# The last pass of a gated product: its weights read once in fp32 and split on the chip

## The chip, the cores and the metric

The kernel runs on one core of a Trainium2 chip. The metric is the device time of one execution in microseconds. Engines: TensorE (PE in the profile; its weight loads are PEld), VectorE (DVE), ScalarE (ACT), GpSimd (POOL) and SyncE (SP), whose queue issues nearly all transfers.

## The reference

Attention over 4 batches of 12 heads, 448 tokens, with the heads mixed before and after the softmax, gives x of 1792 tokens by 768. Then come two layers, everything in fp32:

```python
h = x @ w_in            # w_in: 768 x 2048
g = h - np.tanh(h)
x = g @ w_out           # w_out: 2048 x 768
# second layer: a softmax over tokens and over 32 slots, 8 experts of 768 x 1024 x 768
logits = x @ phi
slot_input = softmax_over_tokens(logits).T @ x
slot_out[e] = np.maximum(slot_input[e] @ w1[e], 0.0) @ w2[e]
out = softmax_over_slots(logits) @ slot_out
```

Inputs arrive as 64-bit words for some weights; the kernel converts `w_in` and `w_out` to fp32 on the chip and keeps them in DRAM as `wi` and `wo`.

## The kernel before, in words

**Stages.** `talking_heads` computes the attention and, beside it, converts the weights. `moe_and_slots` follows. Its stage 1 computes h transposed, 128 columns of `w_in` at a time (16 of them, `NF`), for four passes over the tokens (`PASS`, 512, 512, 512 and 256 tokens). One pair of pass and column block is a *unit* t, 0 to 63; the last pass is units 48 (`LAST`) to 63. The tail after it sums up slots and runs the experts.

**A unit.** `product` (lines 712 to 727) makes hp, 128 by 256 in the last pass, of 6 chunks c of 3 matmuls each (L722). fp32 is split into a rounded part h and a rest l, both in fp32r, for w and for x, and the three matmuls are hw·hx, lw·hx and hw·lx. So a unit needs w as 128 x 2 halves m x 2 parts x 384. In the first pass `split_w` makes the parts of `wi` on the chip (L683 ScalarE, L684 GpSimd) and `save_w` writes both to DRAM as `wis`, 768 KB a unit. The other passes read `wis` back.

**The gate.** `gate_act` (ScalarE: Square L741 into a PSUM bank `sq`, Square L742 into `qd`, Tanh L745 into `g`, Relu L746 into `mk`), `gate_first` (VectorE: L751 and L752 on `qd`, L753 on `g`) and `gate_last` (VectorE: L758 reads `qd` and writes hp, L759 copies hp into `g` under the mask). There is one `qd` and one `mk`; of `g` there are five. VectorE's L751 starts after ScalarE's Relu, since both read the bank `sq`. `turn_g` transposes g on TensorE (L780), a ScalarE copy (L783) takes it out of PSUM.

**The order.** The schedule is written by hand: each engine runs in the order in which the program issues. `step(t)` issues, for t above 2: the load of a later unit; `gate_act(t-1)`, between whose L742 and L745 a function (`beside`) is called; then `product(t)`, with hooks ahead of chunks: chunk 1 `gate_first(t-1)`, chunk 2 `turn_g(t-2)`, chunk 3 and 4 the work on logits and slots of the pass before (steps 49 to 53), chunk 4 `gate_last(t-1)`. The transposes of unit t-2 therefore stand a third of the way into unit t.

**The ring.** `ring` has four slots of 6 KB a partition: two in `rg`, one each in two tiles of a pool that is closed within the last pass (step 54), to make room for three expert homes `z`. Up to unit 47 slot t % 4 is used; `load_w(t + 3)` loads whole units (L674). In the last pass only t % 2 is left, and `load_half(t + 2, m)` (L678) reloads a half of the slot just read, ahead of chunk 3 and behind chunk 5, as soon as TensorE is through with it. Expert tiles of 1.5 MB are loaded into homes that come free; in the last pass they go in pieces, one `load_piece` (L656) a step, behind the halves on SP's queue. The rest is issued behind the last unit, and then homes follow as `give` finds them (L652): the ring, `xc`, the gate's tiles, then each expert tile that is used up.

Of the kernel before, what the change touches and what calls it, by code (L numbers as in the profile page):

```python
# [9 lines left out]
FP32 = mybir.dt.float32  # L10
F32R = mybir.dt.float32r
ACTF = mybir.ActivationFunctionType
ALU = mybir.AluOpType
# [7 lines left out]
PASS = (512, 512, 512, 256)  # L21
# [525 lines left out]
def moe_and_slots(tc, ident, xd, wi, wo, wo4, wis, consts, w1, w2, out, box):  # L547
    nc = tc.nc
    NT, DM = out.shape
    KD = DM // 128  # L550
    NF = len(wi)
# [6 lines left out]
    HALF = DM // 2  # L558
    FH = F1 // 2
    NPASS = len(PASS)  # L560
    NST = NPASS * NF
    TM = max(PASS)
# [9 lines left out]
    RU = 2 * DM  # L572
    GR = 5
    NX = 7
    LAST = NST - NF

    whole = ExitStack()
    firsts = ExitStack()
# [8 lines left out]
    def bank(tag, shape, name):  # L587
        return bank_pool[tag].tile(shape, FP32, tag=tag, name=name)

    def r32(ap):  # L590
        return ap.bitcast(F32R)
# [6 lines left out]
    rg = rgp.tile([128, 2 * RU], FP32, tag="rg", name="rg")  # L598
# [3 lines left out]
    ring = [w.rearrange("p (m h i) -> p m h i", m=2, h=2) for w in (rg[:, :RU], rg[:, RU:], *rgs)]  # L602

    def unit(t):
        return ring[t % 4 if t < LAST else t % 2]


    mem = {}
# [8 lines left out]
    def give(x, last=False):  # L617
        free.append((x, last))
        load_expert()
# [34 lines left out]
    def load_piece(n=1):  # L654
        for dst, src in pending[:n]:
            nc.sync.dma_start(out=dst, in_=src)  # L656
        del pending[:n]
# [10 lines left out]
        return take(("e", t), n)  # L668

    def load_w(t):  # L670
        if t < NF:
            nc.sync.dma_start(out=unit(t)[:, :, 1], in_=wi[t].rearrange("p (m i) -> p m i", m=2))
        elif t < NST:
            nc.sync.dma_start(out=unit(t), in_=wis[t % NF])  # L674

    def load_half(t, m):
        if t < NST:
            nc.sync.dma_start(out=unit(t)[:, m], in_=wis[t % NF][:, m])  # L678

    def split_w(t, eng):  # L680
        if t < NF:
            w = unit(t)
            nc.scalar.activation(out=r32(w[:, :, 0]), in_=w[:, :, 1], func=ACTF.Copy)  # L683
            eng.tensor_tensor(out=r32(w[:, :, 1]), in0=w[:, :, 1], in1=w[:, :, 0], op=ALU.subtract)  # L684

    def save_w(t):
        if t < NF:
            nc.scalar.dma_start(out=wis[t], in_=unit(t))
# [7 lines left out]
    def load_x(p):  # L696
        n = PASS[p]
        if p == NPASS - 1:
            xbuf[p] = mem["thp"].tile([128, XW], FP32, tag="x0", name="xc")
            dst = xbuf[p][:, KD * n:2 * KD * n]  # L700
        else:
            dst = xbuf[p % 2][1][:, :KD * n]
        nc.sync.dma_start(out=dst.rearrange("p (a s) -> p a s", a=KD), in_=xd[p])
# [25 lines left out]
    def temps_of(t):  # L729
        n = PASS[t // NF]  # L730
        if t < 2:
            part = [quad[:, i * n:(i + 1) * n] for i in range(4)]
            return part[0], part[1], part[2], part[3] if t else mem["g0"]
        return mem["sq"][t], mem["qd"][:, :n], mem["mk"][:, :n], mem["g"][t % GR][:, :n]

    def gate_act(t, beside=None):
        hp = hps[t]
        if t > 1:
            mem["sq"] = {t: bank(f"q{t % 2}", [128, PASS[t // NF]], "sq")}
        sq, qd, mk, g = temps_of(t)  # L740
        nc.scalar.activation(out=sq, in_=hp, func=ACTF.Square)  # L741
        nc.scalar.activation(out=qd, in_=sq, func=ACTF.Square, bias=tshift)  # L742
        if beside:
            beside()
        nc.scalar.activation(out=g, in_=hp, func=ACTF.Tanh)  # L745
        nc.scalar.activation(out=mk, in_=sq, func=ACTF.Relu, bias=tlimit, scale=-1.0)  # L746
# [12 lines left out]
        nc.vector.copy_predicated(out=g, mask=mk.bitcast(I32), data=hp)  # L759

    def g_of(t):
        return temps_of(t)[3] if t < 2 else mem["g"][t % GR][:, :PASS[t // NF]]

    turns = [0]

# [25 lines left out]
    def load_o(f):  # L791
        if f < NF:
            nc.sync.dma_start(out=mem["wo"][f % NG], in_=wo[f])
# [45 lines left out]
    def mix_t(b):  # L839
        xt = bank("lg", [128, PASS[b]], "lT")  # L840
        nc.tensor.matmul(xt, lhsT=sel.rearrange("p g s -> p (g s)"), rhs=lp[b], start=True, stop=True)
        lg[b] = xt
# [7 lines left out]
    def slot_exp(b):  # L850
        xt = lg.pop(b)
        nm = keep.tile([128, 1], FP32, tag="nm", name="nm")
        ng = keep.tile([128, 1], FP32, tag="ng", name="ng")
        et = keep.tile([128, TM], FP32, tag="et", name="et")[:, :PASS[b]]
        sb = keep.tile([128, 1], FP32, tag="sb", name="sb")
        a = None
        nc.vector.tensor_reduce(out=nm, in_=xt, op=ALU.max, axis=AX.X)
        if b:
            nc.vector.tensor_tensor(out=nm, in0=nm, in1=run_m, op=ALU.max)
        nc.vector.tensor_scalar(out=ng, in0=nm, scalar1=-1.0, scalar2=None, op0=ALU.mult)  # L860
        nc.scalar.activation(out=et, in_=xt, func=ACTF.Exp, bias=ng, accum_out=sb)
        if b:
            a = keep.tile([128, 1], FP32, tag="al", name="al")
            nc.scalar.activation(out=a, in_=run_m, func=ACTF.Exp, bias=ng)
        es_in[b] = (a, et)
        runs[b] = (nm, sb)
# [59 lines left out]
    for n in range(3, NF + 1):  # L926
        m = 3 if n in (3, 4, 14, 15) else 2
        pieces[n], todo = todo[:m], todo[m:]

    def step(t):  # L930
        b, f = divmod(t, NF)
        hooks = {}

        def on(c, fn, *a):
            hooks.setdefault(c, []).append(lambda: fn(*a))

        if t < LAST:
            if 2 < t < LAST - 1:
                load_w(t + 3)
        else:  # L940
            on(KD // 2, load_half, t + 2, 0)
            on(KD, load_half, t + 2, 1)
        for n, hf in pieces.get(t - 1, []):
            if hf:
                load_o(n + NG)
        if t > 2:
            gate_act(t - 1, lambda: split_w(t + 1, nc.gpsimd))
        else:
            split_w(t + 1, nc.gpsimd)
        u = t - 2  # L950
        ws = pieces.get(t, [])
        if ws:
            on(1, turn_w, *ws[0])
        if t > 2:
            on(1, gate_first, t - 1)
        on(2, turn_g, u)
        if ws:
            on(3, turn_w, *ws[1])
        if b == 0:
            on(1, save_w, t)  # L960
        if b and f == 1:
            on(3, logits, b - 1, NQ - 1)
            on(4, logits_out, b - 1)
        if b and f == 2:
            hooks[1] = [lambda: mix_t(b - 1), lambda: slot_exp(b - 1)] + hooks[1]
            on(3, mix_n, b - 1)
            on(KD, slot_run, b - 1)
            on(KD, gates_first, b - 1)
        if b and f == 3:
            on(4, slot_turn, b - 1)  # L970
            on(KD, gates_last, b - 1)
        if b and f in (4, 5):
            on(3, slot_sum, b - 1, 2 * f - 8, 2 * f - 6)
        if t > 2:
            on(4, gate_last, t - 1)
        if b + 1 < NPASS:
            if f == 6:
                load_x(b + 1)
            if 8 <= f < 8 + KD:
                on(4, split_x, b + 1, f - 8)  # L980
        if len(ws) > 2:
            on(KD - 1, turn_w, *ws[2])
        if t in folds:
            on(KD - 1, fold_first)
            on(KD, fold_last, folds[t])
        if u % NG == NG - 1 and u % NF < NF - 1:
            on(KD, logits, u // NF, u % NF // NG)
        product(t, hooks)
        if b == 1 and f % 2 == 1 and f // 2 < NX:
            give(mem["ex"][f // 2], f // 2 == NX - 1)  # L990
        if b == 1 and f == NF - 1:
            give(mem["thp"].tile([128, EXB], FP32, tag="x1", name="ex"))
        if b == NPASS - 2 and f == NF - 1:
            mem["slow"] = True
            for l in range(2):
                give(xap.tile([128, EXB], FP32, tag=f"x{l}", name="ex"))
        if b == NPASS - 1:
            if f == 6:
                firsts.close()
                zp = whole.enter_context(tc.tile_pool(name="m_z", bufs=1, reuse_waits="tile"))  # L1000
                for i in range(3):
                    give(zp.tile([128, EXB], FP32, tag=f"z{i}", name="ex"))
            load_piece()
# [40 lines left out]
    tmp = temps.enter_context(tc.tile_pool(name="m_tmp", bufs=1, side="right", reuse_waits="tile"))  # L1044
# [2 lines left out]
    xbuf[1] = [thp.tile([128, XW], FP32, tag=f"x{l}", name="xb") for l in range(2)]  # L1047
    mem["SA"] = mids.tile([128, FB], FP32, tag="SA", name="SA")
    mem["ex"] = [mids.tile([128, EXB], FP32, tag=f"ex{i}", name="ex") for i in range(NX)]
    mem["g"] = [tmp.tile([128, TM], FP32, tag=f"g{i}", name="g") for i in range(GR)]  # L1050
    mem["qd"] = tmp.tile([128, TM], FP32, tag="qd", name="qd")
    mem["mk"] = tmp.tile([128, TM], FP32, tag="mk", name="mk")
    mem["wo"] = [mem["ex"][0][:, i * DM:(i + 1) * DM] for i in range(NG)]
# [9 lines left out]
    t = NST  # L1063
# [22 lines left out]
    tmp = whole.enter_context(tc.tile_pool(name="m_tz", bufs=1, side="right", reuse_waits="tile"))  # L1086
# [271 lines left out]
```

## Time and profile before

| | us |
|---|---|
| median of 3 runs | 939.89 |
| lowest, highest | 939.65, 943.64 |
| the profiled execution | 942.47 |
| its span, first to last instruction | 940.7 |

The profile shows one execution. Its rows name a line, an engine, an operation and the program's tiles; times are microseconds from the start of the span unless they are said to be ns. An idle time of an engine carries the event that ended it.

### The profile page before, as it was taken

How to read it: one execution, taken by the hardware profiler on the slowest of the kernel's cores; microseconds unless marked ns; L12 is line 12 of the kernel's file. 1: busy time of each engine (PE TensorE's matmuls, PEld its weight loads, DVE VectorE, ACT ScalarE, POOL GpSimd, SP SyncE). 2: the span in 40 equal slices, each digit the busy share in tenths (PEclk: the TensorE clock that was granted, in tenths of full speed). 3: DMA queues.
4: the chain of work that ended last, by engine and by line, in shares of the span. 5: the costliest groups of instructions: out<-in, count | busy, mean ns of one | idle time of the engine just before them, and what ended most of it. 6: DMA issues, size and time to landing. Idle time of an engine off the chain costs nothing.

```text
span 940.7 us, 19311 instructions
## 1 busy us (share of the span) xinstructions
PE 899.0 (96%) x6926; PEld 659.9 (70%) x6926; DVE 560.4 (60%) x1251; ACT 567.7 (60%) x1283; POOL 265.2 (28%) x467
## 2 busy tenths in 40 slices
PE   8799999999999999999999999999999989799985
PEld 6567777777777777777778777767776767665532
DVE  4376767767677666686555667557766775530103
ACT  4687767767777777777566576545664665521013
POOL 1364445544446444565432222000000000000000
PEclk9999999999999999999999999999999999999987
DMA  6986678976789766795368878669754438999997
GB/s 140 231 224 196 206 212 227 242 217 187 208 229 243 235 183 196 207 249 179 134 222 255 316 239 280 239 252 352 302 201 168 168 123 267 366 394 421 425 388 266
DMA packets 143858, 230.22 MB, mean 245 GB/s; under 512 B 60884, under 2 KB 121364, under 8 KB 139924
## 3 DMA queue, kind: packets, MB, share of 16 engines
q1 hardware_dynamic: 140416, 216.13, 71.4%
q10 hardware_dynamic: 3348, 12.87, 3.5%
q8 instruction: 56, 0.92, 0.4%
q14 instruction: 38, 0.31, 0.1%
HBM read 154.25 MB, written 36.18 MB: 202 GB/s over the span
## 4 chain that ended last, share of the span: by engine, by line
PE 83%; DMA 10%; ACT 2%; DVE 2%; issue 1%; SPq 1%; POOL 0%; ACTq 0%; POOLq 0%; DVEq 0%
PE hp L722 23%; PE pm L297 15%; PE tm L333 14%; PE vx L351 8%; PE sc L266 7%; DMA D<-S 4%; DMA ex<-in_moe_w_dram 3%; PE gt L780 2%; DMA rg<-wis 2%; PE so L1185 2%; PE h L1146 1%; PE lgp L830 1%; PE sp L912 1%; PE wt L799 1%; PE tz L1164 1%
## 5 line engine op out<-in xcount | busy, mean ns | idle before, releaser
L333 PEld LDWEIGHTS tm<-wk,e 120*112 120x112 f32 (+1 forms) x1440 | 174.8, 178 | 71.1 <-issue 59.8
L299 DVE TENSOR_REDUCE mx<-pm 120x1 f32<-120x448 f32 x180 | 112.1, 623 | 133.7 <-PE pm L297 133.2
L297 PE MATMUL pm<-D,wpre 120*120 120x448 f32 x360 | 174.9, 568 | 10.2 <-DMA D<-S 9.7
L336 ACT ACTIVATE aT<-tm 112x480 f32<-112x480 f32 x180 | 105.4, 585 | 123.4 <-PE tm L333 123.4
L333 PE MATMUL tm<-wk,e 120*112 120x120 f32 (+1 forms) x1440 | 177.5, 267 | 1.0 <-POOL wk L323 1.0
L323 POOL TENSOR_SCALAR wk<-wpost,rv 120x120 f32<-120x120 f32 x180 | 125.6, 698 | 142.5 <-PE tm L333 116.9
L722 PE MATMUL hp<-xa,rg 128*128 128x512 f32 x576 | 152.5, 405 | 0.0
L722 PEld LDWEIGHTS hp<-xa,rg 128*128 128x128 f32 x576 | 102.4, 188 | 28.5 <-issue 10.7
L306 ACT ACTIVATE e<-pm,mx 120x448 f32<-120x448 f32 x180 | 113.5, 630 | 6.2 <-DVE rv L318 3.3
L274 ACT ACTIVATE S<-sc 120x448 f32<-120x448 f32 (+1 forms) x186 | 90.8, 544 | 8.3 <-DMA D<-S 3.7
L1157 POOL MEMSET tq<- 128x256 f32 x8 | 2.4, 312 | 315.8 <-PE sip L1125 267.8
L751 DVE SCALAR_TENSOR_TENSOR qd<-qd,sq 128x512 f32<-128x512 f32 (+1 forms) x62 | 38.3, 618 | 83.1 <-ACT mk L746 83.1
L741 ACT ACTIVATE sq<-hp 128x512 f32<-128x512 f32 (+1 forms) x62 | 32.7, 527 | 88.1 <-PE hp L722 88.1
L351 PE MATMUL vx<-aT,vn 112*64 112x120 f32 (+1 forms) x1536 | 84.0, 262 | 0.0
L351 PEld LDWEIGHTS vx<-aT,vn 112*64 112x64 f32 x1536 | 73.9, 137 | 6.2 <-issue 0.9
L297 PEld LDWEIGHTS pm<-D,wpre 120*120 120x120 f32 x360 | 51.4, 182 | 33.3 <-issue 14.3
L722 PE MATMUL hp<-xb,rg 128*128 128x512 f32 x288 | 74.7, 404 | 0.0
L312 POOL TENSOR_SCALAR rv<-ss 120x1 f32<-120x1 f32 x180 | 43.0, 239 | 97.5 <-ACT e L306 87.9
L266 PE MATMUL sc<-khi,qT 64*120 64x448 f32 (+1 forms) x384 | 69.0, 388 | 0.8 <-DVE qT L249 0.8
L68 POOL TENSOR_TENSOR fa<-fa,f 128x384 f32<-128x384 f32 x64 | 65.5, 1024 | 5.3 <-issue 0.2
L722 PEld LDWEIGHTS hp<-xb,rg 128*128 128x128 f32 x288 | 52.0, 188 | 16.6 <-issue 6.3
L722 PE MATMUL hp<-xc,rg 128*128 128x256 f32 x288 | 42.5, 293 | 6.0 <-DMA rg<-wis 6.0
(163 smaller groups left out, 1317.2 us busy)
## 6 DMA issues: line engine op xcount, KB each, us to landing
ex<-in_moe_w_dram SPq DMA_DIRECT2D x25, 1536.0 KB
D<-S SPq DMA_DIRECT2D x172, 210.0 KB
rg<-wis SPq DMA_DIRECT2D x34, 768.0 KB
f<-in_moe_w_in_dram SPq DMA_DIRECT2D x32, 384.0 KB
f<-in_moe_w_out_dram SPq DMA_DIRECT2D x32, 384.0 KB
wis<-rg ACTq DMA_DIRECT2D x16, 768.0 KB
rg<-wis SPq DMA_DIRECT2D x28, 384.0 KB
wi<-fa SPq DMA_DIRECT2D x32, 192.0 KB
```

What stands on the lines that cost most here:

```text
L68: eng.tensor_tensor(out=out, in0=bits(a), in1=bits(p), op=ALU.add)
L266: nc.tensor.matmul(xs[e][0][:ni], lhsT=qT[n][s, l, p, :ni], rhs=kt[s], start=(i == 0), stop=(i == 2))
L274: nc.scalar.activation(out=dst, in_=xs[e][0][:ni], func=ACTF.Copy)
L297: nc.tensor.matmul(x[:r], lhsT=wpre[:r, :m, :], rhs=D_t.pop(s)[:r], start=True, stop=True)
L299: nc.vector.tensor_reduce(out=mx[:r], in_=x[:r], op=ALU.max, axis=AX.X, negate=True)
L306: nc.scalar.activation(out=e[:r], in_=pp_t.pop(s)[:r], func=ACTF.Exp, bias=mx_t.pop(s)[:r], accum_out=ss[:r])
L312: nc.gpsimd.tensor_scalar(out=rv[:r], in0=ss_t.pop(s)[:r], scalar1=EPS, scalar2=None, op0=ALU.add)
L323: nc.gpsimd.tensor_scalar(out=wk[:r], in0=wpost[:r], scalar1=ss_t.pop(s)[:r], scalar2=None, op0=ALU.mult)
L333: nc.tensor.matmul(x[:, c, :, :m], lhsT=e[:r, c * JP:(c + 1) * JP], rhs=wk[:r, :, :m], start=True, stop=True)
L336: nc.scalar.activation(out=attn_t[n][:, :, :, c0:c0 + m], in_=x[:, :, :, :m], func=ACTF.Copy)
L351: nc.tensor.matmul(x[64 * e:64 * e + 64, i, :ni], lhsT=nat_v[b, h // NP][:, h % NP, c, :], rhs=a[:, c, h, :ni], start=(c == 0), stop=(c == ...
L722: nc.tensor.matmul(hp, lhsT=r32(w[:, m, hl, cs]), rhs=r32(x_of(b, c, l)), start=(c == 0 and i == 0), stop=(c == KD - 1 and i == 2))
```

## The change

In the last pass w is loaded as fp32 from `wi`, into the place of the l part, and split per half: half 0 by ScalarE (a Copy to fp32r) between L742 and Tanh of the step before the product, half 1 by VectorE (a copy to fp32r) ahead of chunk 3 of that step; for both halves GpSimd then subtracts in place. Up to unit 54 (below `THREE` = 55) the four slots stay in use and whole units are loaded three steps ahead; from unit 55 there are three slots: the two of `rg` and one in the place of three `g` tiles, and halves are loaded three units ahead. The `g` tiles of the last pass lie in the other two `g` tiles and in the free half of `qd`.

```diff
+    THREE = LAST + 7
     def unit(t):
-        return ring[t % 4 if t < LAST else t % 2]
+        return ring[t % 4] if t < THREE else ring[(4, 0, 1)[(t - THREE) % 3]]
     def load_w(t):
-        if t < NF:
-            nc.sync.dma_start(out=unit(t)[:, :, 1], in_=wi[t].rearrange("p (m i) -> p m i", m=2))
-        elif t < NST:
+        if t == THREE:
+            ring.append(mem["tmp"].tile([128, RU], FP32, tag="gl", name="rg").rearrange(
+                "p (m h i) -> p m h i", m=2, h=2))
+        if t < NF or t >= LAST:
+            nc.sync.dma_start(out=unit(t)[:, :, 1], in_=wi[t % NF].rearrange("p (m i) -> p m i", m=2))
+        else:
             nc.sync.dma_start(out=unit(t), in_=wis[t % NF])
     def load_half(t, m):
         if t < NST:
-            nc.sync.dma_start(out=unit(t)[:, m], in_=wis[t % NF][:, m])
+            nc.sync.dma_start(out=unit(t)[:, m, 1], in_=wi[t % NF][:, m * HALF:(m + 1) * HALF])
+    def split_half(t, m):
+        if LAST <= t < NST:
+            h, l = unit(t)[:, m, 0], unit(t)[:, m, 1]
+            if m:
+                nc.vector.tensor_copy(out=r32(h), in_=l)
+            else:
+                nc.scalar.activation(out=r32(h), in_=l, func=ACTF.Copy)
+            nc.gpsimd.tensor_tensor(out=r32(l), in0=l, in1=h, op=ALU.subtract)
     def g_of(t):
-        return temps_of(t)[3] if t < 2 else mem["g"][t % GR][:, :PASS[t // NF]]
+        if t < 2:
+            return temps_of(t)[3]
+        if t < LAST:
+            return mem["g"][t % GR][:, :PASS[t // NF]]
+        i, n = (t - LAST) % GR, PASS[-1]
+        return mem["qd"][:, n:2 * n] if i == GR - 1 else mem["g"][3 + i // 2][:, i % 2 * n:(i % 2 + 1) * n]
     # in step(t)
-        if t < LAST:
-            if 2 < t < LAST - 1:
-                load_w(t + 3)
-        else:
-            on(KD // 2, load_half, t + 2, 0)
-            on(KD, load_half, t + 2, 1)
+        if 2 < t < THREE:
+            load_w(t + 3)
+        elif t >= THREE:
+            on(KD // 2, load_half, t + 3, 0)
+            on(KD, load_half, t + 3, 1)
-            gate_act(t - 1, lambda: split_w(t + 1, nc.gpsimd))
+            gate_act(t - 1, lambda: split_half(t + 1, 0) if t >= NF else split_w(t + 1, nc.gpsimd))
         on(2, turn_g, u)
+        on(3, split_half, t + 1, 1)
```

The five `g` tiles become slices of two tiles, `gl` (three) and `gh` (two), of the same size in all.

## Rows read from the trace of the kernel before

**Rows 1.** Busy time by stretches: us, PE, PEld, DVE, ACT, POOL, PEclk, DMA share, GB/s
```profile
770.00:828.00 58.00, 48.86 (x389) 40.32 (x388) 34.89 (x90) 30.06 (x83) 0.00 (x0) 1.00 0.89 308
798.00:828.00 30.00, 24.04 (x191) 21.26 (x190) 16.73 (x43) 16.14 (x44) 0.00 (x0) 1.00 0.99 360
840.00:900.00 60.00, 58.92 (x654) 32.73 (x658) 5.37 (x18) 7.61 (x15) 2.12 (x7) 1.00 1.01 423
...
910.00:915.00 5.00, 2.99 (x24) 0.68 (x16) 0.00 (x0) 0.00 (x0) 0.00 (x0) 0.52 1.07 374
```

**Rows 2.** Waits of PE and of ACT, 767 to 829 us: total, times, longest
```profile
PE hp L722 <- DMA rg<-wis: 6.0, 8, 1.5
...
ACT qd L742 <- DVE hp L758: 2.6, 3, 1.3
```

**Rows 3.** Timeline of ACT: start, us, what, idle before and what ended it
```profile
768.34 0.69 ACT L742 ACTIVATE qd<-sq,tshift 128x512 f32<-128x512 f32 x1
...
772.83 0.47 ACT L742 ACTIVATE qd<-sq,tshift 128x256 f32<-128x256 f32 x1 [1.29 <-DVE hp L758]
...
785.33 0.47 ACT L742 ACTIVATE qd<-sq,tshift 128x256 f32<-128x256 f32 x1 [0.96 <-DVE hp L758]
...
794.80 0.48 ACT L742 ACTIVATE qd<-sq,tshift 128x256 f32<-128x256 f32 x1
...
797.92 0.47 ACT L742 ACTIVATE qd<-sq,tshift 128x256 f32<-128x256 f32 x1
798.29 0.38 ACT L745 ACTIVATE g<-hp 128x256 f32<-128x256 f32 x1
...
800.71 0.48 ACT L742 ACTIVATE qd<-sq,tshift 128x256 f32<-128x256 f32 x1 [0.34 <-DVE hp L758]
...
828.81 0.47 ACT L742 ACTIVATE qd<-sq,tshift 128x256 f32<-128x256 f32 x1
```

**Rows 4.** Timeline of PE, one unit that waits for nothing
```profile
795.81 2.38 PE L722 MATMUL hp<-xc,rg 128*128 128x256 f32 x18
```

**Rows 5.** Transfers by form: queue, count, KB each
```profile
rg<-wis SPq DMA_DIRECT2D x28, 384.0 KB
...
ex<-in_moe_w_dram SPq DMA_DIRECT2D x12, 384.0 KB
...
ex<-in_moe_w_dram SPq DMA_DIRECT2D x6, 512.0 KB
```

**Rows 6.** Single lines, duration in ns: least/median/most, or busy us and mean
```profile
L707 ACT ACTIVATE xa<-xa x12: 622/630/653, 483.3 to 670.2; 128x512 fp32r<-128x512 f32 x12
...
L707 ACT ACTIVATE xc<-xc x6: 409/434/435, 731.1 to 755.6; 128x256 fp32r<-128x256 f32 x6
...
L1201 DVE CAST ex<-ceK x1: 391/391/391, 886.3 to 886.3; 128x448 fp32r<-128x448 f32 x1
...
L805 DVE COPY ex<-wt x16: 539/558/565, 509.6 to 594.0; 128x384 f32<-128x384 f32 x16
...
L68 POOL TENSOR_TENSOR fa<-fa,f x64: 1007/1018/1152, 51.4 to 459.0; 128x384 f32<-128x384 f32 x64
...
L51 DVE TENSOR_SCALAR fa<-fa x64: 341/353/1215, 39.9 to 451.7; 128x384 f32<-128x384 f32 x64
```

**Rows 7.** Timeline of DVE
```profile
767.50 0.69 DVE L758 SCALAR_TENSOR_TENSOR hp<-qd,hp 128x512 f32<-128x512 f32 x1
...
799.86 0.41 DVE L753 TENSOR_TENSOR g<-hp,g 128x256 f32<-128x256 f32 x1
800.19 0.42 DVE L758 SCALAR_TENSOR_TENSOR hp<-qd,hp 128x256 f32<-128x256 f32 x1
```

**Rows 8.** The chain that ended last: start, us, what
```profile
882.27 30.49 DMA ex<-in_moe_w_dram
```

**Rows 9.** Timeline of PE in the tail
```profile
912.89 2.79 PE L1185 MATMUL so<-ex,tq 128*32 128x384 f32 x16 [2.01 <-DMA ex<-in_moe_w_dram]
...
924.42 1.50 PE L1185 MATMUL so<-ex,tq 128*32 128x384 f32 x16
```

More of the change, by code (lines that the diff above doesn't have):

```diff
@@ L733, in temps_of @@
             return part[0], part[1], part[2], part[3] if t else mem["g0"]
-        return mem["sq"][t], mem["qd"][:, :n], mem["mk"][:, :n], mem["g"][t % GR][:, :n]
+        return mem["sq"][t], mem["qd"][:, :n], mem["mk"][:, :n], g_of(t)
     def gate_act(t, beside=None):
@@ L1049, in moe_and_slots @@
     mem["ex"] = [mids.tile([128, EXB], FP32, tag=f"ex{i}", name="ex") for i in range(NX)]
-    mem["g"] = [tmp.tile([128, TM], FP32, tag=f"g{i}", name="g") for i in range(GR)]
+    mem["tmp"] = tmp
+    gl = tmp.tile([128, 3 * TM], FP32, tag="gl", name="g")
+    gh = tmp.tile([128, 2 * TM], FP32, tag="gh", name="g")
+    mem["g"] = [gl[:, i * TM:(i + 1) * TM] for i in range(3)] + [gh[:, i * TM:(i + 1) * TM] for i in range(2)]
     mem["qd"] = tmp.tile([128, TM], FP32, tag="qd", name="qd")
```

## The prediction, made before the changed kernel was run

> **What bounds the kernel now.** I read the busy time by stretches first, then who waits for whom in the last pass of stage 1 (767 to 829 us), then the timelines of ScalarE, VectorE and TensorE there, then the end of the chain of waits.
>
> The stretches show a light and a heavy half of the last pass. From 798 to 828 us the DMA engines are busy 99% of the time at 360 GB/s, TensorE only 24.04 of 30 us; afterwards, from 840 to 900 us, DMA stays full at 423 GB/s [rows 1]. The waits name what the product lacks: TensorE stood 6.0 us, in 8 pieces, for ring loads from `wis` [rows 2]. That is what the change can remove from the pass directly.
>
> What is late next is in the same answer. ScalarE's second Square (L742, `qd`) waited three times for VectorE's L758, which reads `qd` last [rows 2]. There is one `qd`, so the gate is a loop: L742, Tanh, Relu on ScalarE, then L751, L752, L753, L758 on VectorE, then L742 of the next unit. The reader is to see the loop alone in ScalarE's timeline: L742 starts at 797.92 and, freed by L758, again at 800.71; so the bare loop takes **2.79 us** [rows 3]. The product itself takes 2.38 us for its 18 matmuls [rows 4]. Before, from the unit at 800.71 to the last at 828.81 (eight units), one unit took 28.10 / 8 = 3.51 us [rows 3]: the loop had 0.72 us to spare, because loads were slower still.
>
> **The change part by part.**
>
> *Loads.* 16 units of 768 KB become 384 KB: 6.3 MB less. Of ring halves and expert pieces, 28 x 384 KB, 12 x 384 KB and 6 x 512 KB are issued from 770 us on [rows 5], 18.87 MB; with the ring halves at 192 KB a unit brings 384 KB and about one piece of 384 to 512 KB, at most 0.92 MB, which 360 GB/s moves in 2.6 us. That is below both the old and the new time of a unit, and the third ring slot gives another unit of lead, so I take TensorE's 6.0 us for loads as gone. If that cover were gone, part of the 6.0 us would return.
>
> *First-half split.* ScalarE's Copy of 128x384 goes between L742 and Tanh, inside the loop. Copies from SBUF to fp32r take 630 ns for 512 columns and 434 for 256 [rows 6], so about 532 for 384. Consecutive operations overlap: L742 lasts 0.47 us, yet Tanh starts 0.37 after it [rows 3]. That takes off 0.10 to 0.11: **0.42 us** (bounds 0.37, the spacing of 256 columns, and 0.53).
>
> *Second-half split.* VectorE's copy stands between L753 and L758, in the loop too. The one cast to fp32r from SBUF takes 391 ns for 448 columns; a copy of 128x384 out of PSUM takes 558 [rows 6]. It is nearest the cast: about 0.36 for 384 columns. L753 lasts 0.41 and L758 starts 0.33 later [rows 7], so 0.08 comes off: **0.28 us** (bounds 0.26 and 0.48).
>
> *Subtractions.* GpSimd has two a unit of 128x384, 1.02 us each [rows 6], 2.04 in all, and nothing else. The first ends some 2.0 us after L742 starts, before the product wants that half; the second starts after VectorE's copy, about 3.1, and ends about 4.2, while TensorE, which waits for the gate (3.9) before its transposes, reaches that half's remainder near 4.7. I cost both at nothing; the cover is 0.5 us for the second. If it went, each microsecond beyond would be TensorE's.
>
> *Queues.* SP's loads per unit stay two or become one; they are behind the same TensorE events and carry the same expert pieces behind them. ScalarE's Tanh and Relu, and so all of VectorE's gate, are queued behind the Copy: that is the 0.42. L758 and the masked copy behind VectorE's copy: the 0.28. The extra ring slot is the old `g0` to `g2`, whose last readers run at step 49, while the load into it is issued at step 52: nothing. The first `z` home waits for unit 54, its piece is due at step 56: nothing.
>
> *The sum for the pass.* The loop becomes 2.79 + 0.42 + 0.28 = **3.49 us**, against 3.51 as loads paced it: the gain is spent. It also binds where the old pass was not short of data. L742 at 768.34 had 0.1 us to spare (L758 of the unit before ended at 767.50 + 0.69 = 768.19 [rows 7]), so 0.6 of 0.70 shows; at 772.83 it already waited for L758 (0.70 more) [rows 3]; after the logits ScalarE has to wait, before the next unit's gate, for VectorE's part of `gates_first`, which is queued behind one more copy, 0.28; and at 785.33 again a wait for L758 brings 0.70 [rows 3]. Sum 2.3 us. So L742 of unit 53, before at 794.80, comes at 797.1; nine spacings of 3.49 give 828.5 and the last gate, with no split behind it, 2.79 more: 831.3, against 828.81 before [rows 3]. **The pass ends 2.5 us later.** With 0.37 and 0.26 it is 1.9, with 0.53 and 0.48 it is 6.6.
>
> *The tail.* It is a stream of expert tiles. The chain ends through a tile issued at 882.27 that lands 30.49 us later [rows 8]; TensorE waits 2.01 us for it at 912.89, and the granted clock in 910 to 915 is 0.52, that is 1.2 GHz, after that idle time [rows 1, 9]. Homes for this stream open where the pass ends (the ring, `xc`, the gate's tiles are given out behind the last unit), so its start moves with the pass. What the lighter loads give is the backlog: 18.87 MB issued less 58 us x 308 GB/s = 17.86 moved by 828 [rows 1, 5] leaves 1.0 MB, 2.5 us at 400 GB/s. Bounds 0 and 2.5; I take 1.0, since a first transfer issued at the end of the pass doesn't flow at once, while a backlog covers that time.
>
> *Total:* 2.5 - 1.0 = **+1.5 us**. The profiled execution took 942.47 us (span 940.7, 1.8 around it), 2.6 above the median 939.89; it would become 944.0, the median **941.4**.
>
> **The rivals.**
>
> *A, slower: the copies cost their upper bounds.* Price: 6.6 - 1.0 = 5.6, 945.5 us. For it: the PSUM copy's 558 ns. Against: the cast's 391 [rows 6]. It decides from a VectorE copy of about 0.55 us on.
>
> *A', slower: VectorE's copy meets GpSimd's subtraction.* A one-input VectorE operation of 128x384 between SBUF operands, L51, has median 353 ns and once took 1215 [rows 6], in the stage where GpSimd works beside it. If each copy lost those 0.86 us, twelve loop-bound units would lose 10.3 more, 951.7 us. It decides if the first subtraction still runs when the copy's turn comes, 2.7 us after L742 starts; with 1.02 us it ends at 2.0, so I give this little. The Trainium skill, SBUF — State Buffer, section "SBUF: two separate sides", says that VectorE in a two-port mode and GpSimd take a port pair exclusively, for a whole instruction. By that rule, the long L51 is explained and the margin of 0.7 us is what protects this change; no row before shows a cast beside a subtraction.
>
> *B, a little faster: the tail's stall goes.* If the stream gains the 2 us that the tile at 912.89 is late, TensorE keeps 2.4 GHz: 2.0 us, and two groups of 16 matmuls take 1.50 instead of 2.79 us each [rows 9]: 4.6 less, 2.5 - 4.6 = -2.1, 937.8 us. Against it: 1.0 MB of backlog is barely enough.
>
> *C, clearly faster: the splits don't lengthen the loop.* Then loads and loop give 2.79 us a unit: ten from 794.80 end at 822.7 instead of 828.81, -6.1, with the backlog -7.1, 932.8 us. For it: ScalarE and VectorE each idle half of the pass. Against: idle time inside a loop is no room, and the order places both copies in it.
>
> *D: the change does not do what it says.* Loads stay late (latency, not bytes, set them). Then the old waits add to the loop only in part; it would end like A.
>
> **How the numbers follow.** Forecast 0.58, A and D 0.15, A' 0.04, B 0.14, C 0.09. A measurement here can tell about 0.5%, 4.7 us: 935.2 to 944.6. Faster by more: C and a third of B, 0.14. Slower: A, A', D and a small part of the forecast's upper end, 0.21. Same: 0.65. The range takes in B's 937.8 and A's 945.5 with a microsecond for each: 936.5 to 946.5; it leaves out C, A' and little else. The forecast's own range is 939 to 945.
>
> **What the profile after would show.** Right: no TensorE wait for ring loads after 798 us; DMA clearly below full there; L742 waiting for L758 in nearly every unit and spaced 3.4 to 3.6 us; TensorE standing for the gate (L759) before its transposes; the pass ending 2 to 3 us later; a wait for an expert tile near the end still there. Wrong: L742 spaced under 3.2 us or without that wait (C), VectorE's copies over 0.5 us (A) or some over 1 us (A'), or the granted clock staying at 2.4 GHz through the last `so` matmuls (B).

## The result and the profile after

| | before | after |
|---|---|---|
| median of 10 runs, us | 940.55 | 945.87 |
| lowest, highest | 936.45, 944.95 | 942.14, 949.67 |
| the profiled execution | 942.47 | 946.25 |
| its span | 940.7 | 944.4 |
| first to last product matmul of the last pass | 767.5 to 828.1: 60.6 | 770.1 to 835.5: 65.4 |
| behind it, to the end of the span | 112.6 | 108.9 |

The ratio of the times is **1.0054**, interval 1.0033 to 1.0076: 5.1 us slower, between 3.1 and 7.1 (the medians themselves lie 5.3 apart). The range 936.5 to 946.5 holds the 945.87; the forecast of 941.4 was 4.5 too low. It had added 1.5 us to a median of 939.89 of three runs, so as a forecast of the change alone it was 3.8 too low.

The two profiled executions differ ahead of the change too: the first product matmul of stage 1 starts at 490.3 us in one and at 492.8 in the other, and over all profiles of this study that start lies between 486.7 and 498.3, though no kernel differs there. So I compare the *pass*, the time from the first start of a product matmul on `xc` to the last, and not the spans. The pass took 4.8 us longer, about the whole loss.

The diff moves lines: L722 is now L735, L742 is L755, L745 L758, L758 L771, L759 L772, L780 L798, L783 L801, L830 L848, L859 L877, L893 L911, L912 L930, and L1185 L1206. The split's lines are L694 (VectorE), L696 (ScalarE) and L697 (GpSimd).

TensorE's product of the pass, by tile (count: least, median and most ns, first and last start):

```profile
L735 PE MATMUL hp<-xc,rg x288: 274/282/685, 770.1 to 835.5; 128*128 128x256 f32 x144
```

**Waits of TensorE after**, 760 to 840 us (total, times, longest):

```profile
PE gt L798 <- DVE g L772: 9.8, 12, 2.4
...
PE gt L798 <- ACT qd L755: 1.1, 1, 1.1
PE gt L798 <- DVE qd L772: 1.1, 1, 1.1
...
PE hp L735 <- POOL rg L697: 0.7, 1, 0.7
```

The 6.0 us for ring loads [rows 2] are gone from this list. In their place TensorE stands before the transposes for the gate. The same answer for the kernel before has, besides the loads:

```profile
PE gt L780 <- DVE g L759: 2.6, 3, 1.2
...
PE gt L780 <- ACT g L745: 1.8, 1, 1.8
```

The wait was not removed, it was exchanged: 6.0 for loads against 7.6 more for the gate (9.8, 1.1 and 1.1 against 2.6 and 1.8; `qd L772` is the gate of a unit whose g lies in the free half of `qd`) and 0.7 for a subtraction. What made the gate late stands in ScalarE's waits of the same stretch: `qd` waited 3 times and 2.6 us for VectorE [rows 2], now 12 times and 10.2.

```profile
ACT qd L755 <- DVE hp L771: 10.2, 12, 1.9
```

**ScalarE's timeline after** (start, us, what, the idle time before it and what ended it) shows the loop at its new length:

```profile
771.51 0.69 ACT L755 ACTIVATE qd<-sq,tshift 128x512 f32<-128x512 f32 x1 [0.66 <-DVE hp L771]
...
801.85 0.47 ACT L755 ACTIVATE qd<-sq,tshift 128x256 f32<-128x256 f32 x1
...
805.31 0.47 ACT L755 ACTIVATE qd<-sq,tshift 128x256 f32<-128x256 f32 x1 [0.37 <-DVE hp L771]
...
808.78 0.48 ACT L755 ACTIVATE qd<-sq,tshift 128x256 f32<-128x256 f32 x1 [0.69 <-DVE hp L771]
...
812.26 0.47 ACT L755 ACTIVATE qd<-sq,tshift 128x256 f32<-128x256 f32 x1 [0.68 <-DVE hp L771]
...
836.17 0.47 ACT L755 ACTIVATE qd<-sq,tshift 128x256 f32<-128x256 f32 x1
```

From unit 53 to unit 62 they come every 3.46 to 3.48 us (one of 3.75 apart), each freed by L771; the last, behind which no split stands, comes after 2.81. Against the pass's own start, `qd` of unit 53 stands at 31.8 us here (801.85 - 770.1), 27.3 before (794.80 - 767.5, [rows 3]): **of the 4.8 us, 4.5 are there by unit 53**, and from there on the two kernels run nearly level, one paced by the loop, the other by its loads.

**Busy time by stretches after** (us, PE, PEld, DVE, ACT, POOL, PEclk, DMA share, GB/s) locates the loss. DMA in the second half is at 0.76, where it was at 0.99 [rows 1]; and in the first half the granted clock isn't 1.00:

```profile
770.00:798.00 28.00, 21.68 (x154) 16.54 (x153) 18.09 (x45) 15.02 (x39) 11.05 (x11) 0.94 0.43 141
798.00:835.00 37.00, 30.45 (x248) 25.63 (x247) 23.40 (x63) 22.51 (x63) 20.18 (x20) 1.00 0.76 246
...
776.00:778.00 2.00, 0.50 (x5) 0.53 (x5) 1.32 (x2) 1.31 (x4) 1.35 (x2) 0.98 0.95 349
778.00:780.00 2.00, 2.00 (x13) 0.75 (x11) 1.72 (x5) 0.81 (x2) 0.85 (x2) 0.50 0.09 30
780.00:782.00 2.00, 2.00 (x12) 1.36 (x9) 0.51 (x2) 0.60 (x1) 0.80 (x1) 0.67 0.00 0
```

From 778 to 780 us TensorE runs at 0.50, that is 1.2 GHz. Its timeline shows what it did before, and what the fall did:

```profile
772.33 0.63 PE L798 MATMUL gt<-ident,g 128*128 128x128 f32 x4 [1.38 <-DVE g L772]
...
777.50 0.70 PE L798 MATMUL gt<-ident,g 128*128 128x128 f32 x4 [2.42 <-DVE g L772]
...
778.77 1.94 PE L848 MATMUL lgp<-g,wphi 128*32 128x512 f32 x8
...
790.51 0.86 PE L735 MATMUL hp<-xc,rg 128*128 128x256 f32 x5 [0.70 <-POOL rg L697]
792.49 0.41 PE L798 MATMUL gt<-ident,g 128*128 128x128 f32 x2 [1.11 <-ACT qd L755]
...
793.81 0.62 PE L930 MATMUL sp<-tq,es 128*32 128x512 f32 x1 [0.56 <-ACT tq L801]
```

TensorE stood 2.42 us for the gate, and the eight `lgp` matmuls behind it took 1.94 us. Before, the eight took 1.06. TensorE's timeline before, with the rows that answer the last two above (the `sp` matmuls, which sum up slots, waited for nothing):

```profile
774.57 1.06 PE L830 MATMUL lgp<-g,wphi 128*32 128x512 f32 x8
...
785.86 0.41 PE L780 MATMUL gt<-ident,g 128*128 128x128 f32 x2 [1.24 <-DVE g L759]
...
786.77 0.62 PE L912 MATMUL sp<-tq,es 128*32 128x512 f32 x1
```

**VectorE and GpSimd after, single rows.** The casts and copies are as long as each other to a few ns, the two busy groups first; then two VectorE operations that got longer, with the subtraction beside each:

```profile
L694 DVE CAST rg<-rg x16: 348/350/351, 770.5 to 832.6; 128x384 fp32r<-128x384 f32 x16
...
L696 ACT ACTIVATE rg<-rg x16: 512/514/516, 766.9 to 830.3; 128x384 fp32r<-128x384 f32 x16
...
783.68 1.01 POOL L697 TENSOR_TENSOR rg<-rg 128x384 fp32r<-128x384 f32 x1 [2.88 <-ACT rg L696]
...
784.26 0.45 DVE L877 TENSOR_TENSOR nm<-nm,run_m 128x1 f32<-128x1 f32 x1
...
792.93 1.00 POOL L697 TENSOR_TENSOR rg<-rg 128x384 fp32r<-128x384 f32 x1 [0.26 <-ACT rg L696]
792.97 1.10 DVE L911 TENSOR_TENSOR ceK<-ceK,cs 128x128 f32<-128x128 f32 x1
```

The same two operations before, when GpSimd did nothing in the pass:

```profile
778.87 0.16 DVE L859 TENSOR_TENSOR nm<-nm,run_m 128x1 f32<-128x1 f32 x1
...
786.35 0.29 DVE L893 TENSOR_TENSOR ceK<-ceK,cs 128x128 f32<-128x128 f32 x1
```

**TensorE in the tail after.** It still waits for expert tiles near the end [rows 9], but in this execution every group of 16 `so` matmuls stays at 1.47 to 1.50 us:

```profile
918.68 1.50 PE L1206 MATMUL so<-ex,tq 128*32 128x384 f32 x16 [1.42 <-DMA ex<-in_moe_w_dram]
...
922.81 1.50 PE L1206 MATMUL so<-ex,tq 128*32 128x384 f32 x16 [1.04 <-DMA ex<-in_moe_w_dram]
```

### The profile page after: what moved, and what is told of

Same layout as the page of the kernel before. It is cut to its first block, busy times and chain, and to the rows that moved or that the text cites. A ratio compares the mean times of both kernels' runs of the same rounds, so it can differ in the third digit from the quotient of the medians.

```text
span 944.4 us, 19437 instructions
## 1 busy us (share of the span) xinstructions
PE 897.8 (95%) x6926; PEld 660.0 (70%) x6926; DVE 565.8 (60%) x1267; ACT 572.6 (61%) x1299; POOL 297.7 (32%) x499
## 4 chain that ended last, share of the span: by engine, by line
PE 81%; DMA 8%; ACT 4%; DVE 3%; issue 2%; POOL 1%; SPq 0%; ACTq 0%; POOLq 0%; DVEq 0%
PE hp L735 22%; PE pm L297 14%; PE tm L333 13%; PE vx L351 8%; PE sc L266 6%; DMA D<-S 5%; PE gt L798 2%; PE h L1167 2%; DMA ex<-in_moe_w_dram 2%; PE so L1206 2%; PE lgp L848 1%; PE sp L930 1%; PE tz L1185 1%; PE wt L817 1%; DMA kn<-in_k_dram 1%
## 5 line engine op out<-in xcount | busy, mean ns | idle before, releaser
L735 PE MATMUL hp<-xa,rg 128*128 128x512 f32 x576 | 152.5, 405 | 0.0
L735 PEld LDWEIGHTS hp<-xa,rg 128*128 128x128 f32 x576 | 102.4, 188 | 28.5 <-issue 10.7
L697 POOL TENSOR_TENSOR rg<-rg 128x384 fp32r<-128x384 f32 x32 | 32.2, 1008 | 216.2 <-PE gt L798 182.0
L735 PE MATMUL hp<-xb,rg 128*128 128x512 f32 x288 | 74.7, 404 | 0.0
L735 PEld LDWEIGHTS hp<-xb,rg 128*128 128x128 f32 x288 | 52.0, 188 | 16.6 <-issue 6.3
L755 ACT ACTIVATE qd<-sq,tshift 128x512 f32<-128x512 f32 (+1 forms) x62 | 39.3, 634 | 11.9 <-DVE hp L771 10.2
```

The costliest lines, as they stand in the source:

```text
L735: nc.tensor.matmul(hp, lhsT=r32(w[:, m, hl, cs]), rhs=r32(x_of(b, c, l)), start=(c == 0 and i == 0), stop=(c == KD - 1 and i == 2))
```

## The experiments

My theory: the lighter loads work, and the loop through the one `qd`, lengthened by two copies, spends what they give; the rest of the loss is the early part of the pass. The rivals: the subtractions or ports, not the loop, make units 3.47 us long; the loads' bytes did not matter; the loss is in the tail. Every run below is one row of this table. "Unit" is the spacing of `qd` from unit 53 on, "fall" the granted clock of the pass's first 15 us where it fell there, "loads" TensorE's waits for the ring; ratios are to the kernel before of the same group of runs.

| run | pass, us | unit, us | fall | loads, us | ratio, interval |
|---|---|---|---|---|---|
| before | 60.6 | 3.51 | no | 6.0 | 1 |
| changed kernel | 65.4 | 3.47 | .89 | 0 | 1.0054 (1.0033, 1.0076) |
| the same again | 65.3 | 3.47 | .89 | 0 | 1.0041 (1.0011, 1.0071) |
| two `qd` | 60.5 | 3.15 | no | 0 | 0.9956 (0.9925, 0.9986) |
| two `qd` again | 62.0 | 3.14 | .89 | 0 | 1.0030 (0.9999, 1.0060) |
| no split | 55.2 | 2.78 to 3.14 | no | 0 | 0.9974 (0.9938, 1.0010) |
| copies alone | 65.0 | 3.47 | .89, and .89 in the second | 1.3 | 1.0017 (0.9996, 1.0039) |
| matmuls in the wait | 67.4 | 3.47 | .89 in the second 15 us | 0 | 1.0070 (1.0040, 1.0099) |
| split from unit 55 | 60.9 | 3.47 | no | 0 | 1.0003 (0.9974, 1.0031) |
| from 55, two `qd` | 58.0 | 3.14 | no | 0 | 0.9980 (0.9954, 1.0006) |
| ring alone | 55.3 | 2.78 to 3.13 | no | 0 | 0.9961 (0.9930, 0.9991) |
| ring alone again | 55.8 | 2.79 to 3.12 | no | 0.5 | 0.9976 (0.9946, 1.0005) |
| ring, two `qd` | 55.3 | 2.5 and 3.1 by turns | no | 0.4 | 0.9962 (0.9931, 0.9993) |
| half the bytes alone | 55.7 | 2.79 to 3.14 | no | 0.9 | 0.9963 (0.9933, 0.9993) |

### The changed kernel once more

> The changed kernel once more. Loop theory (the two copies stand in the gate's loop through the one qd): L755 spaced 3.47 us from unit 53 on, the last pass (first to last product matmul on xc) 65 to 66 us, ratio to the kernel before 1.003 to 1.008. Clock theory (TensorE's wait of 2.4 us before the transposes of unit 47 lets the granted clock fall): the eight logits matmuls behind it take 1.9 us again and the clock in the stretch around them is under 0.8. Rival (that fall was a chance of one execution): they take 1.06 us and the pass is 1.5 us shorter.

Pass 65.3, units 3.47 us, the clock falling at the same place: the early loss is no accident of one profile.

### Is the loop the pace? A second `qd`, and no split

```diff
-        return mem["sq"][t], mem["qd"][:, :n], mem["mk"][:, :n], g_of(t)
+        qd = mem["mk"][:, n:2 * n] if t >= LAST and t % 2 else mem["qd"][:, :n]
+        return mem["sq"][t], qd, mem["mk"][:, :n], g_of(t)
```

> Odd units of the last pass use a second qd, in the free half of mk; all copies, subtractions and loads stay. Loop theory: the spacing falls from 3.47 to about 2.85 us (now the loop through mk: Relu 0.47, six VectorE operations 2.33, changeovers), the pass to 59.5 to 61 us, ratio to the kernel before 0.996 to 1.001. Rival (GpSimd's subtractions or late loads set the pace): spacing stays above 3.3 us, pass above 64, ratio 1.003 or more.

ScalarE's timeline with two `qd` (odd units in `mk`'s free half): no wait for VectorE ahead of the Square, and units about 3.15 us apart.

```profile
801.52 0.47 ACT L756 ACTIVATE qd<-sq,tshift 128x256 f32<-128x256 f32 x1
...
804.69 0.47 ACT L756 ACTIVATE mk<-sq,tshift 128x256 f32<-128x256 f32 x1
...
807.81 0.47 ACT L756 ACTIVATE qd<-sq,tshift 128x256 f32<-128x256 f32 x1
```

So the loop through `qd` was the pace, but only 0.32 us of it could be had: the next limit follows at once. It is the way from a product's end through its gate to its transposes, which stand two units later in TensorE's order; the copies lie on that way too, and TensorE still waits for the gate there. TensorE's and ScalarE's timelines show one round of it:

```profile
808.69 0.41 PE L799 MATMUL gt<-ident,g 128*128 128x128 f32 x2 [0.60 <-DVE g L773]
...
810.56 0.37 ACT L755 ACTIVATE sq<-hp 128x256 f32<-128x256 f32 x1 [0.95 <-PE hp L735]
```

The first Square of unit 55 starts at 804.28, its transposes, freed by its gate, at 808.69, and the first Square of unit 57, freed by the product behind these transposes, at 810.56: 6.28 us for two units, 3.14 each. I had expected 2.85 us a unit.

In this run TensorE's timeline has the same wait before the transposes, and *no* fall behind it:

```profile
776.04 0.63 PE L799 MATMUL gt<-ident,g 128*128 128x128 f32 x4 [2.39 <-DVE g L773]
...
776.95 1.06 PE L849 MATMUL lgp<-g,wphi 128*32 128x512 f32 x8
```

```diff
-            gate_act(t - 1, lambda: split_half(t + 1, 0) if t >= NF else split_w(t + 1, nc.gpsimd))
+            gate_act(t - 1, lambda: split_w(t + 1, nc.gpsimd))
-        on(3, split_half, t + 1, 1)
```

(and the product reads the unsplit weights for both parts in the last pass; that line is left out here)

> The last pass leaves the split out (both copies, both subtractions) and multiplies with the unsplit weights for both parts; the light loads stay. Loop theory: spacing 2.79 us, first part as in the kernel before, pass 55 to 57 us, ratio 0.988 to 0.995. Rival (loads are late by latency, whatever their bytes): TensorE waits for ring loads again, pass 59 us or more, ratio 0.996 or more.

Without the split the pass takes 55.2 us, and most units come 2.78 to 2.81 us apart. ScalarE's timeline:

```profile
805.56 0.47 ACT L755 ACTIVATE qd<-sq,tshift 128x256 f32<-128x256 f32 x1 [0.34 <-DVE hp L771]
...
807.97 0.37 ACT L754 ACTIVATE sq<-hp 128x256 f32<-128x256 f32 x1 [1.02 <-PE hp L735]
808.37 0.47 ACT L755 ACTIVATE qd<-sq,tshift 128x256 f32<-128x256 f32 x1
```

That is the length of the bare loop of the prediction, but L771 frees `qd` in only three of the ten units behind unit 53, as at 805.56. In the others, as at 807.97, ScalarE waits for the product: four units of TensorE took 11.51 us from 803.15 on, of which it stood 0.80 for the gate, so its own work is 2.7 us a unit, nearly as long as the loop. With the same ring and the same bytes, the split's operations together cost 10.2 us of pass (65.4 - 55.2). The ratio, 0.9974, followed less than I had expected.

### The copies without the change

```diff
+    def pad_copy():
+        nc.scalar.activation(out=r32(mem["pad"][0]), in_=..., func=ACTF.Copy)
-            gate_act(t - 1, lambda: split_w(t + 1, nc.gpsimd))
+            gate_act(t - 1, lambda: pad_copy() if LAST + 2 < t + 1 < NST else split_w(t + 1, nc.gpsimd))
+        if LAST + 2 < t + 1 < NST:
+            on(3, lambda: nc.vector.tensor_copy(out=r32(mem["pad"][1]), in_=...))
```

(on the kernel before; the targets, two `pad` tiles, are halves of the `g` tiles that the last pass leaves unused, the source is `SA`, into which the slots are summed; the lines that lay out these tiles are left out here)

> The kernel before with its loads from wis, and from unit 51 on one ScalarE and one VectorE copy of 128x384 on unused space, at the places where the change puts them; nothing reads them. Loop theory: spacing at least 3.49 us, L742 waiting for L758 in most units while some waits for loads remain, pass 61.5 to 63.5 us, ratio 1.001 to 1.004. Rival (the copies fit into idle time of the two engines, the cost lies with subtractions and the order of loads): pass 60 to 61 us as before, ratio 0.999 to 1.001.

```profile
805.15 0.47 ACT L742 ACTIVATE qd<-sq,tshift 128x256 f32<-128x256 f32 x1 [0.69 <-DVE hp L758]
...
808.61 0.47 ACT L742 ACTIVATE qd<-sq,tshift 128x256 f32<-128x256 f32 x1 [0.70 <-DVE hp L758]
```

ScalarE's timeline shows 3.46 us a unit with no GpSimd operation at all: the two copies alone make the loop's length, the subtractions add nothing to it. Load waits fell to 1.3 us, though every byte was still loaded: a loop of 3.46 us hides most of them. The pass was longer than I had expected, 65.0 against 61.5 to 63.5, and two falls of the clock (0.89 in the first and in the second 15 us) stand in it, the first behind a wait of 1.79 us, the second behind one of 2.11. A wait of 1.80 us at the place of the first had no fall behind it in the kernel before.

### The early part: matmuls in the wait, and a later start

```diff
+        for _ in range({LAST - 2: 9, LAST - 1: 18}.get(t, 0)):
+            nc.tensor.matmul(x[:, 0, :], lhsT=ident, rhs=ident, start=True, stop=True)
```

(ahead of the transposes of units 46 and 47, into the bank that these then fill)

> The changed kernel, with 9 and 18 small matmuls ahead of the transposes of units 46 and 47, in the bank that the transposes then overwrite, where TensorE stood 1.4 and 2.4 us. Clock theory (the wait lets the granted clock fall, and that costs what the prediction had not counted): clock 1.00 through the first 15 us of the pass, the logits matmuls back at about 1.06 us, the pass 63.5 to 64.2 instead of 65.4 us, ratio to the kernel before 1.001 to 1.006. Rival (the matmuls are slow there for another reason, or the gate's chain covers it): pass 65 to 65.6.

The `lgp` matmuls were back at 1.06 us, so the fall at that place was prevented. But the added matmuls took longer than the wait they were to fill, TensorE's timeline (18 instructions, 36 rows of the trace):

```profile
772.90 4.18 PE L798 MATMUL gt<-ident 128*128 128x128 f32 x36
```

and the clock fell 15 us later instead, behind waits of 0.70, 1.12 and 0.55 us within 4 us, which the changed kernel has there too and without a fall (window of this run):

```profile
792.00:794.00 2.00, 2.00 (x12) 0.39 (x8) 1.93 (x6) 0.00 (x0) 0.53 (x1) 0.50 0.00 0
```

The pass was 67.4 us. The run shows that the fall can be moved, not that its price can be had back.

```diff
-        if t < NF or t >= LAST:
+        if t < NF or t >= THREE:
-        if LAST <= t < NST:
+        if THREE <= t < NST:
```

> As the change, but the split begins with unit 55; one qd. Loop theory: unit 53's L755 27.3 us after the pass begins, then 3.47 us a unit, pass 60.8 to 61.8 us, no fall of the clock in the first part; ratio to the kernel before 0.996 to 1.002. Rival (the early units don't matter, the pass is paced from the end): pass 65.

With the split only from unit 55 on, units still take 3.47 us from there, and `qd` of unit 53 stands at 27.3 us as it did before the change. The pass is 60.9: the 4.5 us are wholly the early part's, and a loop of 3.47 costs next to nothing against loads that paced 3.51.

> Second qd, and units 48 to 54 loaded whole and already split from wis; the split begins with unit 55. Loop theory: first part as in the kernel before (unit 53's L755 27.3 us after the pass begins, against 31.75 with the change), then 3.15 us a unit as with two qd: pass 58 to 59 us, ratio 0.990 to 0.996. Rival (768 KB a unit is late in the first part too, now that the ring is whole): TensorE waits for ring loads, pass 60 or more.

Both edits together: 58.0 us, 2.6 shorter than before. The time followed only in part, 0.9980, and the interval reaches 1.

### The loads: bytes or ring?

The ring of the change with the whole 768 KB of `wis`, and no split:

```diff
-        if t < NF or t >= LAST:
+        if t < NF:
-            nc.sync.dma_start(out=unit(t)[:, m, 1], in_=wi[t % NF][:, m * HALF:(m + 1) * HALF])
+            nc.sync.dma_start(out=unit(t)[:, m], in_=wis[t % NF][:, m])
```

(the lines that take the split out, as above, are left out here)

> The change's ring (four slots, then three) without the split: 768 KB a unit from wis to the end, one qd. Bytes theory (a unit and its expert piece are 1.2 MB, which the DMA engines move at 360 to 400 GB/s): spacing 3.0 to 3.4 us, some waits for ring loads left, pass 57.5 to 59.5 us, and the tail keeps its backlog; ratio 0.994 to 1.000. Depth theory (two slots made the loads late, not their bytes): no waits for loads, spacing 2.79, pass 55 to 56. Third: depth gives nothing, pass 60 or more.

No wait for the ring, though DMA was nearly full, as the window shows (its last two numbers):

```profile
798.00:823.00 25.00, 23.47 (x193) 21.27 (x192) 16.52 (x43) 15.92 (x45) 0.00 (x0) 1.00 0.95 354
```

And the other half, the kernel before with its two slots and half the bytes (no split):

```diff
-            nc.sync.dma_start(out=unit(t)[:, m], in_=wis[t % NF][:, m])
+            nc.sync.dma_start(out=unit(t)[:, m, 1], in_=wi[t % NF][:, m * HALF:(m + 1) * HALF])
```

(`load_w` does the same for whole units, and the product reads the unsplit weights for both parts; these lines are left out here)

> The kernel before with its two slots and only the fp32 weights loaded in the last pass (half the bytes); the split is left out, both parts are the unsplit weights. Bytes theory (half the bytes alone end the waits for loads): no such waits, spacing 2.79, pass 55 to 56 us, ratio 0.993 to 0.999. Depth theory (a load issued one and a half units ahead is late whatever its size): waits for ring loads of 2 us or more remain, pass 57 to 60 us.

TensorE's waits and the window of this kernel:

```profile
PE hp L722 <- DMA rg<-wi: 0.9, 2, 0.5
```

```profile
798.00:823.00 25.00, 23.31 (x190) 20.96 (x189) 16.36 (x42) 15.65 (x44) 0.00 (x0) 1.00 0.92 299
```

**Either part alone takes nearly all of the 6.0 us**, and each alone brings the pass to within 0.6 us of both together (55.2). The change pays for the second with 10 us of split.

> The deeper ring without the split, and the second qd. Loop theory: the gate's next limit is the way from the end of a product over its gate to its transposes, two units later, about 2.7 us a unit; 1.2 MB in 2.7 us are 440 GB/s, more than the 423 seen, so loads come back as the limit: spacing 2.7 to 2.9, pass 53.5 to 55.5 us, ratio 0.992 to 0.997. Rival (the freed qd gives the full step, loads keep up): pass under 53.

> The deeper ring without the split once more, with more rounds. Pass 55.3 us as before; if the median follows the pass (5.3 us shorter than in the kernel before), ratio 0.992 to 0.997. Rival (the tail is a stream that ends when it ends): ratio 0.998 or more.

> The change with a second qd, once more. Its pass was 60.5 us, as the kernel before has it, yet the ratio was 0.9956. If the median follows the pass: ratio 0.998 to 1.001. Rival (light loads leave the tail a gain of its own of 3 to 4 us, clock falls aside): ratio 0.994 to 0.997 again.

The ring alone is faster than the kernel before in its first group of runs, 0.9961 (0.9930 to 0.9991), and so than the changed one; in its second group, 0.9976, the interval reaches 1. A second `qd` adds nothing that shows (0.9962): once the copies are out, the loop is late in only a few units, and TensorE's own work is nearly the pace. The two `qd` on the changed kernel came out at 0.9956 and at 1.0030, whose intervals don't meet; its second profile had the clock's fall and a pass 1.5 us longer. Why 7 us lie between the two groups stays open.

## Why the prediction was right and wrong

**Right: the loop.** I had forecast 3.49 us a unit, and 3.47 was measured; the Copy added 0.41 us (forecast 0.42) and VectorE's cast 0.27 (0.28). That the gain of the loads is spent there is shown by the no-split run (about 2.8) and by the copies alone (3.46 without the rest of the change). Rival C, that the splits don't lengthen the loop, falls with that; so does rival A's dear copy, since every cast took 348 to 351 ns.

**Right in effect, incomplete in cause: the loads.** The waits went, as forecast. But the prediction had them go by bytes, and the third slot as an extra; the ring-alone run has all the bytes, 0.95 of DMA, and no wait. Full DMA engines beside a wait for a load [rows 1] didn't mean that the engines lacked throughput: the load was issued too late for its size. Rival D asked for lead rather than bytes; the two runs show that either nearly suffices, and the change brings both.

**Wrong: the early part, 4.5 us instead of 2.3.** The four steps of that sum came nearly as written: against the start of the pass, the delay of `qd` grows by 0.6 at unit 47, 0.7 at 48, 0.7 at 51, and at 50 by 0.27 for the cast. What it left out are three terms:

- *The clock, about 1.5 us.* I took the delay of each gate as delay of the next, and did not ask what TensorE does while it waits longer. From `qd` of unit 48 to that of unit 49 the changed kernel took 6.03 and, once more, 6.05 us, the kernel before 4.50. The two profiles of the two-`qd` kernel tell the clock from the rest: 6.05 with the fall, 4.51 without, and 1.5 us between their passes. Without the fall its `qd` of unit 53 came 2.5 us later than before, near the 2.3 of the sum (its second `qd` makes that a comparison at a distance).
- *What else is queued behind the Copy on ScalarE, 0.4.* Under *Queues* I counted Tanh and Relu, and with them VectorE's gate. Behind Relu stands the copy that takes the transposes out of PSUM (L801), and at unit 52 the `sp` matmuls need it at once. It starts 1.41 us behind the second Square (791.96) where it started 1.00 behind it before (785.33, [rows 3]). So TensorE stood 0.56 us for it (793.81), and the `sp` matmuls came 1.32 us after the transposes instead of 0.91. From `qd` of unit 51 to that of unit 52 it took 5.47 us, before 5.07. The run of the copies alone has the same 1.32 without any subtraction.
- *A VectorE operation beside a subtraction, 0.29.* L877 took 0.45 us instead of 0.16 on the way of the logits, ahead of `qd` of unit 50. Rival A' had the mechanism and named the wrong victim: none of the 16 casts met a subtraction, but two operations with two SBUF inputs did, and L911 went from 0.29 to 1.10 us, the length of the subtraction beside it (off the path that sets the end). The Trainium skill, SBUF — State Buffer, section "SBUF: two separate sides", counts VectorE operations with two SBUF inputs among those that lock the ports, against a GpSimd operation that reads SBUF. The trace agrees with that on L911, whose end, 794.07, is 0.14 us behind the subtraction's. I had applied the rule to the operations that the change adds, and not to those that it puts GpSimd beside.

ScalarE's copy of the second term in its timeline, after and before:

```profile
793.37 0.40 ACT L801 ACTIVATE tq<-gt 128x256 f32<-128x256 f32 x1
```

```profile
786.33 0.39 ACT L783 ACTIVATE tq<-gt 128x256 f32<-128x256 f32 x1
```

The three terms make 2.2 us, the whole excess over the forecast. The later start (60.9) shows that the excess belongs to the early units; the clock's part rests on two profiles of one kernel, and the run that was to give it back did not. The other two are read from rows and were not undone one by one.

The subtractions' own time, costed at nothing, cost nothing, though not by the cover that I gave the first: TensorE did stand 0.70 us for one (790.51), but its transposes right behind stood another 1.11 for the gate (792.49), so without that wait they would have begun no earlier.

**Held, but partly by luck: the range.** Its upper end came from rival A's dear copies, and no copy was dear; what filled it were the terms above, which I had at nothing. The bounds of the pass were not worked out evenly either: 1.9 scales the loop alone, and with the early steps scaled too they are 1.6 and 6.4, not 1.9 and 6.6. And the long L51, for which rival A' was given 0.04, was not one case: twelve of the 64 took 0.88 us or more.

**Not settled: the tail, -1.0 us.** In the profiled pair the tail is 3.7 us shorter. The kernel before had a fall of the clock there, which lengthened two groups of `so` matmuls ([rows 9] and the row at 917.93) by 2.5 us together, and the changed kernel had none. The window and the timeline of the kernel before:

```profile
910.00:911.00 1.00, 0.89 (x8) 0.00 (x0) 0.00 (x0) 0.00 (x0) 0.00 (x0) 0.62 1.06 373
```

```profile
917.93 2.74 PE L1185 MATMUL so<-ex,tq 128*32 128x384 f32 x16
```

The 1.2 us that are left are near the forecast, but they are one pair. Falls in the tail stand in the profiles of about half of the kernels of this study, whatever their pass. The seven profiles without one have tails of 108.9 and 109.5 us behind passes of 65 (the changed kernel), and of 110.5 and 111.1 behind passes of 55.3 (the two ring runs), so the tail seems to give something back; whether for the longer pass or for the lighter loads these profiles don't separate. The medians can't tell: 5.1 us, with 3.1 and 7.1 as bounds, fits a pass 4.8 longer with 1.0 given back and with nothing given back. In the other direction a shorter pass isn't paid in full either: 5 us less of pass gave 2.3 to 4.9 us of median (no split, ring, half the bytes), which fits a tail that waits for its stream of expert tiles.

I had also put the tail's fall behind the 2.01 us that TensorE stood for the tile at 912.89, and rival B on it. The window above shows the clock at 0.62 before that wait, with the `so` matmuls running; and two `qd` stood 2.25 us for a tile there without a fall. So rival B's clock is seen in the pair, but not its reason: the waits for tiles stayed (1.42 and 1.04 us).

The kernel came out slower, to which I had given 0.21. The bounds that I gave the unknown costs all concerned the copies' durations, while what failed was what stands behind them in the early units.

## What to carry to other kernels

When two engines pass one buffer to and fro, its round trip is the pace, however idle both engines look; price each added operation against that loop and the next limit behind it, not against busy shares. A wait for a load beside full DMA engines may be a matter of how early it is issued: try more lead and fewer bytes separately before paying compute for either. Behind an operation that is added to an engine, list everything queued there, also what is not of the loop. Before GpSimd work is added to a stage, list the VectorE operations already there with two SBUF inputs, and before TensorE is made to wait longer, count a fall of its clock among the outcomes.

## What was not expected of the hardware

Waits of 2.4 us before the same transposes were followed by a fall to 1.2 GHz in three executions (the changed kernel twice, two `qd` again) and not in a fourth (two `qd`, 2.39 us). At 1.76 to 1.80 us one execution of nine fell (copies alone, 1.79); the kernel before (1.80) and seven others didn't. So the wait's length alone did not tell. At this place a fall lengthened the way from `qd` of unit 48 to that of unit 49 by 1.3 us (copies alone) to 1.5. One spacing of 3.75 us late in the pass stands in every kernel with the split and one `qd` (at unit 57, or 59 where the split begins with unit 55), and not in the copies alone; its cause stays open.
